# Loads held behind crossbar transposes in a block-sparse attention and MLP-mixer kernel, and two more head pairs turned by the crossbar

## The chip, the cores and the metric

The kernel runs on one core of one Trainium2 chip. The metric is the device time of one execution in microseconds; of several executions the median is taken. TensorE is called PE, VectorE DVE, ScalarE ACT, GpSimd POOL and SyncE SP, as in the profile.

## The reference

The first part is attention over 4 batches of 8 heads, 768 positions and a head size of 64. Positions are grouped in 24 blocks of 32. A query block sees its neighbours, the first and last block, and three sampled blocks; the first and last query block see everything.

```
scores = q @ k.T / 8                      # per batch and head, 768 x 768
scores = where(mask, scores, -1e9)
attn   = softmax(scores)                  # over the keys
x      = concat over heads of attn @ v    # 4 x 768 x 512
```

The second part is a mixer on x: a token step over the 768 positions with 256 hidden units, then a channel step over the 512 channels with 1536 hidden units.

```
u   = x + (relu(x.T @ w_tok1) @ w_tok2).T
out = u + relu(u @ w_ch1) @ w_ch2         # 4 x 768 x 512, float32
```

## The kernel before

The work is cut into 16 **pairs** of heads (pair p has heads 2p and 2p+1; four pairs are a batch). The scores of a pair are made in nine steps: three blocks of 256 queries (t) by three blocks of 256 keys (jj). In a step PE makes the scores of both heads (`ps`, L678), ACT takes their exponential into `et` (L688), and PE multiplies `et` with the values, to which a column of ones is appended (`po`, L772). After the third key block DVE takes the reciprocal of the sum and writes the normalised rows into `x` (L786, L787). In pairs 0 to 3 the mask is added to the scores by 24 additional rows of the operands; from pair 4 on (`NT0`) DVE multiplies `et` by a 0/1 `mask` instead (L696), and the two heads sit in the two halves of the partitions.

There are two score buffers (`ps`), one `po`, seven `et` (`NET`) and three general PSUM buffers (`pm`).

**q and k have to be turned** so that the head dimension lies on the partitions. The rows land in "homes" (`homes`, `load_pair`, L254, DMAs issued by POOL), DVE brings each into the order that the turn wants (`relayout`, L567; v is copied at L564), and then there are two ways. Pairs 1 to `NPE` - 1 are turned by PE against an identity (`transposes`, L620), and DVE or ACT copies the result from PSUM (L634, L649). Later pairs are turned by the DMA crossbar, issued by SP (`crossbar`, L589). With `NPE = 8` pairs 8 to 15 go by crossbar, and their relayouts are planned after `all_loaded`, the landing of the last load. Each turned pair lives in one of four buffers (`NV`) of `ktb` and `qtb`.

**The mixer** runs per batch and half of the channels (g): `tok` (PE L849, L874; DVE L882) and then a turn of u for the channel step, `turn_by_crossbar` (L829, issued by SP). Batch 0 is done pair by pair in `tok_pair` (L909, L932, L940) and turned by PE (L955, evacuated at L966). The channel step is `ch`: its first layer in L989 with the relu on ACT or DVE (L813, L815), its second in L1016, added to u at L1028 and written by SP at L1041.

**The order on each engine** is written by a planner at build time. `Planner` keeps a clock and a list of streams of PE work with priorities (`P.stream`; a lower number goes first) and of single operations (`P.op`) with planned costs. It issues whatever is ready by its own clock. On the chip each engine then runs its instructions in that order, and an instruction waits for its semaphores, with all behind it on that engine. The queue of loads, `pull`, puts POOL's DMAs in order in the same way: pairs 4 to 15 one after the other, `load_ch1` and `load_ch2` after pairs 5 and 7, and the copies that spread the mask (`spread_mask`, L534). From pair 4 on `qk_stream` issues two steps in one visit when it can, which takes two free `ps` buffers and two free `et`.

The head of the program has "filler" matmuls (`idle_mm`, L316), which compute nothing that is used: seven at the start and four of 512 columns just ahead of the first scores.

## Time and profile before

| | us |
|---|---|
| median of 5 executions | 256.38 (255.88 to 257.86) |
| the profiled execution's own time | 257.86 |
| its span, first to last instruction | 255.8 |
| PE busy in it | 247.4 |
| ACT, DVE busy | 176.9, 177.2 |
| POOL busy | 50.1 |

The profile is of one execution, the slowest of the five. Its page gives the busy time of each engine, then the span in 40 slices of 6.4 us, each digit a busy share in tenths. The groups of instructions have the mean duration of one and the idle time ahead of it. [...] what one costs in a row is read from the chain of waits, where a piece "x4" gives the time of four in a row. A timeline line has the start in us, the duration, engine, line, operation, and in brackets the idle time before it and what ended it.

### The profile page before, as it was taken

To read this page: it belongs to the slowest core of one execution; us is meant where nothing else is said; L and a number is where in the kernel's file an instruction comes from. 1 tells how busy PE (TensorE), PEld (TensorE's weight loads), DVE (VectorE), ACT (ScalarE), POOL (GpSimd) and SP (SyncE) were. 2 spreads that over 40 slices of the span, in tenths; PEclk is the share of its full clock that TensorE was granted. 3 is DMA by queue.
4 is the path that set the end of the run, shared out by engine and by line. 5 is a ranking of instruction groups with operands and counts; after the bars stand their busy time and mean duration, and the time that the engine had idled before them with its cause. 6 is when DMAs were issued, how large, how long until landed. Compare 5 with 4: busy or idle time off the path is not lost.

```text
span 255.8 us, 6662 instructions
## 1 busy us (share of the span) xinstructions
PE 247.4 (97%) x2784; PEld 161.2 (63%) x2804; DVE 177.2 (69%) x392; ACT 176.9 (69%) x223; POOL 50.1 (20%) x84
## 2 busy tenths in 40 slices
PE   8899999899999999999999999999999999999995
PEld 2589989656666556656766666557567544556444
DVE  6788968799988988998998998897883113200122
ACT  6699999898989676778978777768775620177100
POOL 8845989477200000000000000000000000000000
PEclk9999999999999999999999999999999999999999
DMA  6999999999947442457050202310410302200123
GB/s 147 196 215 201 213 202 205 203 202 200 201 75 145 79 105 82 61 148 105 3 112 14 62 3 64 82 50 37 103 46 0 64 37 86 109 16 0 41 87 121
DMA packets 43326, 26.36 MB, mean 103 GB/s; under 512 B 23776, under 2 KB 40432, under 8 KB 43296
## 3 DMA queue, kind: packets, MB, share of 16 engines
q0 software_dynamic: 15104, 12.98, 32.0%
q1 hardware_dynamic: 27920, 12.76, 20.2%
q8 instruction: 22, 0.36, 0.6%
q10 hardware_dynamic: 272, 0.20, 0.3%
q14 instruction: 8, 0.07, 0.1%
HBM read 26.74 MB, written 6.29 MB: 129 GB/s over the span
## 4 chain that ended last, share of the span: by engine, by line
PE 89%; DVE 7%; ACT 2%; issue 1%; DVEq 0%; ACTq 0%
PE pm_ch L989 25%; PE pm_ch L1016 24%; PE ps L678 15%; PE po L772 14%; PE pm_tok L874 3%; PE pm_tok L849 3%; PE ps_idle L316 2%; ACT et L688 2%; DVE x L940 1%; DVE et L696 1%; PE pm_tok_p L909 1%; DVE x L787 1%; DVE qlay L567 0%; DVE ktb L634 0%; DVE qtb L419 0%
## 5 line engine op out<-in xcount | busy, mean ns | idle before, releaser
L688 ACT ACTIVATE et<-ps 128x1024 bf16<-128x1024 f32 x144 | 138.9, 1023 | 32.7 <-PE ps L678 30.2
L989 PE MATMUL pm_ch<-uT,w_ch 128*128 128x384 bf16 x384 | 72.1, 326 | 0.0
L696 DVE TENSOR_TENSOR et<-et,mask 128x1024 bf16<-128x1024 bf16 x108 | 69.6, 683 | 0.6 <-ACT et L688 0.6
L1016 PE MATMUL pm_ch<-w_ch,rc 128*128 128x512 bf16 (+2 forms) x292 | 65.9, 362 | 1.1 <-issue 0.5
L772 PEld LDWEIGHTS <-et 128*128 128x128 bf16 x1152 | 49.0, 97 | 17.2 <-issue 2.8
L772 PE MATMUL po<-vaug,et 128*128 128x65 bf16 x1152 | 55.9, 193 | 1.1 <-ACT et L688 0.4
L678 PE MATMUL ps<-qtb,ktb 64*128 64x256 bf16 (+1 forms) x576 | 55.2, 273 | 1.7 <-ACT et L688 1.4
L813 ACT ACTIVATE rc<-pm_ch 128x384 bf16<-128x384 f32 x65 | 32.0, 492 | 25.1 <-PE pm_ch L989 25.0
L989 PEld LDWEIGHTS <-w_ch 128*128 128x128 bf16 x384 | 34.4, 97 | 20.7 <-issue 2.3
L1028 DVE TENSOR_TENSOR o<-pm_ch,x 128x512 f32<-128x512 f32 x23 | 15.9, 690 | 45.1 <-PE pm_ch L1016 45.0
L1016 PEld LDWEIGHTS <-rc 128*128 128x128 bf16 x312 | 27.6, 98 | 25.6 <-issue 1.9
L678 PEld LDWEIGHTS <-ktb 64*128 64x128 bf16 (+1 forms) x576 | 29.5, 95 | 18.8 <-issue 13.7
L787 DVE TENSOR_TENSOR x<-po,recip 128x256 bf16<-128x256 f32 x48 | 20.4, 424 | 1.7
L815 DVE TENSOR_SCALAR rc<-pm_ch 128x384 bf16<-128x384 f32 x31 | 17.1, 553 | 3.0 <-PE pm_ch L989 2.4
L786 DVE RECIPROCAL recip<-po 128x4 f32<-128x4 f32 x48 | 8.6, 180 | 14.4 <-PE po L772 13.7
L882 DVE TENSOR_TENSOR x<-pm_tok,x 128x512 bf16<-128x512 f32 x18 | 11.8, 684 | 3.6 <-PE pm_tok L874 3.4
L874 PE MATMUL pm_tok<-a_t,w_tok 128*128 128x256 bf16 x72 | 10.8, 277 | 0.0
L849 PE MATMUL pm_tok<-x,w_tok 128*128 128x256 bf16 x72 | 9.5, 273 | 0.0
L874 PEld LDWEIGHTS <-w_tok 128*128 128x128 bf16 x72 | 7.5, 128 | 1.7 <-issue 1.1
L534 POOL COPY mask<-maskb 128x240 bf16<-128x240 bf16 (+1 forms) x18 | 8.1, 516 | 0.0
L254 POOL DMA_DIRECT2D vraw<-in_v_dram x10 | 7.5, 750 | 2.9 <-DMA w_ch<-in_moe_w_ch_dram 1.1
L849 PEld LDWEIGHTS <-w_tok 128*128 128x128 bf16 x72 | 6.4, 97 | 1.1 <-issue 0.4
(101 smaller groups left out, 137.2 us busy)
## 6 DMA issues: line engine op xcount, KB each, us to landing
out_dram<-o SPq DMA_DIRECT2D x17, 256.0 KB, 2.0
w_ch<-in_moe_w_ch_dram POOLq DMA_DIRECT2D x8, 384.0 KB, 9.9
vraw<-in_v_dram POOLq DMA_DIRECT2D x10, 192.0 KB, 7.4
kraw<-in_k_dram POOLq DMA_DIRECT2D x9, 192.0 KB, 8.8
qraw<-in_q_dram POOLq DMA_DIRECT2D x9, 192.0 KB, 7.6
out_dram<-o SPq DMA_DIRECT2D x13, 128.0 KB, 2.0
w_tok<-in_moe_w_tok_dram POOLq DMA_DIRECT2D x2, 384.0 KB, 9.7
ktb<-in_v_dram POOLq DMA_DIRECT2D x3, 192.0 KB, 7.3
```

The costliest lines, as they stand in the source:

```text
L678: nc.tensor.matmul(out=ps[:, hd, 256 * i : 256 * i + 256], lhsT=ktb[n][rows, h, 256 * jj + 128 * i : 256 * jj + 128 * i + 128], rhs=qtb[n] ...
L688: nc.scalar.activation(out=et[:, :, :], in_=ps[:, :, :], func=AF.Exp, scale=0.125)
L696: nc.vector.tensor_tensor(out=ets[s][:, :, :].rearrange("k h (i q) -> k h i q", i=2), in0=ets[s][:, :, :].rearrange("k h (i q) -> k h i q" ...
L772: nc.tensor.matmul(out=po[:, hd, c, :], lhsT=et[:, hd, 256 * i + 128 * c : 256 * i + 128 * c + 128], rhs=va[:, hd, 2 * jj + i, 0:65], star ...
L787: nc.vector.tensor_tensor(out=free(xs[b][:, pb // 2, 2 * t, 128 * (pb % 2) : 128 * (pb % 2) + 128], 0, [[64, 2], [256, 2], [1, 64]],), in0 ...
L813: nc.scalar.activation(out=o(), in_=i, func=AF.Relu)
L815: nc.vector.tensor_scalar(out=o(), in0=i, scalar1=0.0, scalar2=None, op0=ALU.max)
L849: nc.tensor.matmul(out=box["pm"][:, t, :], lhsT=w_tok1[:, sc, 128 * t : 128 * t + 128], rhs=xs[b][:, g, sc, :], start=(t == 0 and sc == 0) ...
L874: nc.tensor.matmul(out=ubox["pm"][:, i, :], lhsT=w_tok2[:, t, :, 2 * s2 + i], rhs=a_t[:, t, :], start=(i == 0 and t == 0), stop=(i == 1 an ...
L989: nc.tensor.matmul(out=pbox["pm"][:, 0:384], lhsT=w_ch1[:, dmc, 128 * cc : 128 * cc + 128], rhs=st[b]["uT"][:, dmc // 2, 3 * sh : 3 * sh + ...
L1016: nc.tensor.matmul(out=pbox["pm"][:, 0:n], lhsT=box["rc"][:, cc, 128 * sc : 128 * sc + 128], rhs=w_ch2[:, cc, lo : lo + n], start=(cc == 0 ...
L1028: nc.vector.tensor_tensor(out=o[:, :].rearrange("p (g e) -> p g e", g=2), in0=pbox["pm"][:, :].rearrange("p (g e) -> p g e", g=2), in1=st[ ...
```

## The change

- `NPE` goes from 8 to 6: pairs 6 and 7 are turned by the crossbar too.
- `all_loaded` goes. In its place are `GATES`: behind the loads of pair 7, and again behind those of pair 12, POOL reads one element of each of the two buffers that the crossbar of pair 7 (and 11) writes (`gate`), so that later loads wait for it. The third entry of the table makes no read. Relayouts of a crossbar pair are planned 2 us after the planned end of the loads ahead of the next gate (`quiet`). From pair 9 on a relayout is also planned after the scores of the pair three before.
- SP's planned cost of a crossbar turn goes from 900 to 1300 ns, and what follows it from 5000 to 4600.
- `qk_stream` visits two steps at once only when `mixing()` holds, which is when batch 0 is turned and the channel step can begin.
- The last half of batch 1's u (b = 1, g = 1) is turned by PE and copied from PSUM, not by the crossbar.
- `tok_pair` of pairs 0 to 2 gets a higher priority (stream 2.5 to 1.7, operations 2.2 to 1.5).
- The four fillers of 512 columns ahead of the first scores become eight of 128.

```
--- before.py
+++ after.py
@@ -196,7 +196,8 @@
     NV = 4
     NR = 4
     NET = 7
-    NPE = 8
+    NPE = 6
+    GATES = {7: 7, 11: 12, NP - 1: NP - 1}
     NT0 = 4
 
     sb1 = ctx.enter_context(tc.tile_pool(name="sb1", bufs=1))
@@ -312,10 +313,10 @@
 
     idle_ps = psS.tile([128, 2, 512], FP32, tag="ps", name="ps_idle")
 
-    def idle_mm():
+    def idle_mm(n=512):
         nc.tensor.matmul(
-            out=idle_ps[:, 0, :], lhsT=free(one[:, 0:1], 0, [[0, 128]]),
-            rhs=free(one[:, 0:1], 0, [[0, 512]]), start=True, stop=True,
+            out=idle_ps[:, 0, 0:n], lhsT=free(one[:, 0:1], 0, [[0, 128]]),
+            rhs=free(one[:, 0:1], 0, [[0, n]]), start=True, stop=True,
         )
 
     for i in range(7):
@@ -424,8 +425,8 @@
     first_lay(acopy, "k", 0)
     e2a, e2b = e2_mm(0, psM, "pm"), e2_mm(0, psO, "po")
     kt0 = first_turn("k", 0)
-    for i in range(4):
-        idle_mm()
+    for i in range(8):
+        idle_mm(128)
     first_evac(acopy, "q", 0, 0, qt0)
     first_evac(acopy, "q", 0, 1, qt0)
     e2_copy(acopy, 0, 0, e2a)
@@ -551,7 +552,8 @@
     kT_there, qT_there, va_there, qk_done, pv_done = {}, {}, {}, {}, {}
 
     copied = {}
-    all_loaded = Ev()
+
+    quiet = [Ev() for _ in GATES]
 
     def relayout(p):
         lays = {}
@@ -575,7 +577,9 @@
             if nm != "v" and p >= 3:
                 deps.append(qT_there[p - 2, 1])
             if nm != "v" and p >= NPE:
-                deps.append(all_loaded)
+                deps.append(quiet[sum(p > g for g in GATES)])
+            if nm != "v" and p > NV + 4:
+                deps.append(qk_done[p - NV + 1])
             lays[nm + "ev"] = P.op(("dve",), {"dve": 320.0}, deps, emit, prio=2 if nm != "v" else 3)
             copied[nm, p] = lays[nm + "ev"]
         va_there[p] = lays["vev"]
@@ -591,7 +595,7 @@
                     in_=lays[nm][:, :, :, :].rearrange("p c h d -> p (c h d)"),
                 )
             deps = [lays[nm + "ev"], mask_there, qk_done[p - NV]]
-            ev = P.op(("sp",), {"sp": 900.0}, deps, emit, prio=1, lat=5000.0)
+            ev = P.op(("sp",), {"sp": 1300.0}, deps, emit, prio=1, lat=4600.0)
             there[p, 0], there[p, 1] = ev, ev
 
     def transposes(p):
@@ -733,7 +737,7 @@
 
 
             visit = [s]
-            if todo and (todo[0][1:] != (0, 0) or (todo[0][0], 1) in qT_there):
+            if todo and (todo[0][1:] != (0, 0) or (todo[0][0], 1) in qT_there) and mixing():
                 visit.append(todo.pop(0))
             evs = [(Ev(), Ev()) for _ in visit]
 
@@ -888,13 +892,40 @@
             alias(rel, ev)
             u_evs.append(ev)
         alias(a_rel, last)
-        turn_by_crossbar(b, g, u_evs)
+        if (b, g) != (1, 1):
+            turn_by_crossbar(b, g, u_evs)
+            return
+
+        for dmc in (2 * g, 2 * g + 1):
+            last, rel, tbox = Ev(), Ev(), {}
+            for sc in range(NC):
+                def emit(sc=sc, dmc=dmc, rel=rel, tbox=tbox):
+                    if sc == 0:
+                        P.take("pm", rel)
+                        tbox["pt"] = psM.tile([128, NC, 128], BF16, tag="pm", name=f"pm_ut_{b}_{dmc}")
+                    nc.tensor.matmul(
+                        out=tbox["pt"][:, sc, :],
+                        lhsT=st[b]["u"][:, g, sc, 128 * (dmc % 2) : 128 * (dmc % 2) + 128],
+                        rhs=ident[:, :], start=(sc == 0), stop=(sc == NC - 1), is_transpose=True,
+                    )
+                yield 56.0, [u_evs[sc // 2]], [("pm", 1)] if sc == 0 else [], emit, last if sc == NC - 1 else None
+
+            def evac(eng, dmc=dmc, tbox=tbox):
+                o, i = st[b]["uT"][:, g, :, dmc % 2, :], tbox["pt"][:, :, :]
+                if eng == "act":
+                    nc.scalar.copy(out=o, in_=i)
+                else:
+                    nc.vector.tensor_copy(out=o, in_=i)
+
+            ev = P.op(("dve", "act"), {"dve": 555.0, "act": 740.0}, [last], evac, prio=0.5)
+            alias(rel, ev)
+            alias(st[b]["uT_there"][dmc], ev)
 
     def tok_pair(p):
 
         g, cols = p // 2, slice(128 * (p % 2), 128 * (p % 2) + 128)
 
-        urgent = 0.5 if p == 3 else 2.2
+        urgent = 0.5 if p == 3 else 1.5
         box = {}
         last, rel = Ev(), Ev()
         for sc in range(NC):
@@ -1071,11 +1102,12 @@
     P.stream(0, qk_stream())
     P.stream(1, pv_stream())
     P.stream(2, tr_stream())
-    P.stream(2.5, first_tok_stream((0, 1, 2)))
+    P.stream(1.7, first_tok_stream((0, 1, 2)))
     P.stream(0.5, first_tok_stream((3,)))
     P.stream(3, tok_stream())
     P.stream(4, ch_stream())
     P.stream(1.8, mask_stream())
+
 
 
     loads = deque()
@@ -1087,6 +1119,17 @@
             loads.append(load_ch2)
         if 5 <= p <= 7:
             loads.append(spread_mask(p - 5))
+        for gate, behind in GATES.items():
+            if p == behind:
+                loads.append(("gate", gate))
+    gate_t = {"t": 0.0}
+    gates_seen = []
+    seen = sb1.tile([1, 2], BF16, name="seen")
+
+    def gate(p):
+        for i, buf in enumerate((ktb, qtb)):
+            nc.gpsimd.tensor_copy(out=seen[0:1, i : i + 1], in_=buf[p % NV][0:1, 0, 0:1])
+        gate_t["t"] = qT_there[p, 1].t
 
 
     tenant = {n: n for n in range(NR)}
@@ -1101,7 +1144,17 @@
     def pull():
         while loads:
             x = loads[0]
-            if callable(x):
+            if x == ("gate", NP - 1):
+                quiet[-1].t = dma["free"] + 2.0 * US
+            elif isinstance(x, tuple):
+                still = [e for e in quiet if e.t is None]
+                if still and x not in gates_seen:
+                    still[0].t = dma["free"] + 2.0 * US
+                    gates_seen.append(x)
+                if (x[1], 1) not in qT_there or qT_there[x[1], 1].t is None:
+                    return
+                gate(x[1])
+            elif callable(x):
                 if maskb_there.t is None:
                     return
                 x(max(P.now, maskb_there.t))
@@ -1113,10 +1166,8 @@
                 if not free_from:
                     return
                 t, home = min(free_from)
-                load_pair(x, t, home)
+                load_pair(x, max(t, gate_t["t"]), home)
                 tenant[home] = x
-                if x == NP - 1:
-                    all_loaded.t = arrive["v", x].t
             loads.popleft()
 
     while P.streams or P.ops:
```

## Prediction

> I call step p.k the k-th (0 to 8) of the nine score blocks of pair p; four score matmuls make one step. "V" is the po matmuls, "cut" the multiplication of et with the mask.

> **What bounds the kernel now.** First the page's busy line and its slices of the span.

> ```profile
> PE 247.4 (97%) x2784; PEld 161.2 (63%) x2804; DVE 177.2 (69%) x392; ACT 176.9 (69%) x223; POOL 50.1 (20%) x84
> ...
> PE   8899999899999999999999999999999999999995
> ...
> DVE  6788968799988988998998998897883113200122
> ACT  6699999898989676778978777768775620177100
> ```

> TensorE looks full throughout, but a busy PE isn't PE at its peak, so I cut the span where the mixer's channel matmuls begin (54.4 us) and where the last scores are issued (188.4).

> ```profile
> 0.00:54.40 54.40, 50.50 (x742) 40.63 (x744) 44.01 (x118) 47.41 (x54) 41.13 (x72) 1.00 1.17 198
> 54.40:188.40 134.00, 132.54 (x1645) 84.06 (x1661) 118.30 (x249) 105.50 (x123) 9.01 (x13) 1.00 0.46 90
> 188.40:253.50 65.10, 64.36 (x407) 36.49 (x405) 14.93 (x27) 24.03 (x47) 0.00 (x0) 1.00 0.16 53
> ```

> The columns are length, then PE, PEld, DVE, ACT and POOL busy, clock, DMA share, GB/s. After 54.4 PE is 99% busy and the others are not: there the kernel is worth what PE has to issue. Before that I price PE's work by start-to-start spacing from the chain of waits: a score matmul 0.11 us in pairs 0 to 3 (x4 in 0.44) and 0.068 later (x8 in 0.54), a V matmul 0.031 (x16 in 0.49), a 128-column one 0.055 (x6 in 0.34), a 384-column one 0.1625 (x96 in 15.60). Up to 54.4 this makes about 41 us, so PE has slack, while ACT is busy 94% between 12 and 50. The timeline of ACT:

> ```profile
> 45.89 1.94 ACT L688 ACTIVATE et<-ps 128x1024 bf16<-128x1024 f32 x2 [0.68 <-PE ps L678]
> 47.71 0.39 ACT L813 ACTIVATE a_t_p<-pm_tok_p 128x256 bf16<-128x256 f32 x1
> 48.36 1.94 ACT L688 ACTIVATE et<-ps 128x1024 bf16<-128x1024 f32 x2 [0.26 <-PE ps L678]
> 50.19 0.81 ACT L634 COPY qtb<-tq 128x768 bf16<-128x768 bf16 x1
> 50.87 5.88 ACT L688 ACTIVATE et<-ps 128x1024 bf16<-128x1024 f32 x6
> ```

> Exponentials follow each other at 0.97 us except around pair 4, where ACT waits twice for double score visits (0.68, 0.26) and runs two copies. So **the first 54 us are set by exponentials and what delays them, the rest by PE's remaining work**. What counts is how much PE work is left when the mixing begins. The chain there:

> ```profile
> 54.45 0.67 PE ps L678 x8
> 55.11 0.43 PE pm_ch L989 x2
> 55.55 0.24 PE po L772 x8
> 55.79 1.46 PE pm_ch L989 x9
> 57.25 0.54 PE ps L678 x8
> ```

> By counting score matmuls (176 before 54.3), the first line is steps 4.8 and 5.0, the last 5.1 and 5.2: 57.25 is my reference point. Last, the start:

> ```profile
> 5.61 1.91 PE L316 MATMUL ps_idle<-one 128*128 128x512 bf16 x4
> 7.31 1.06 PE L678 MATMUL ps<-qtb,ktb 88*128 88x256 bf16 x4
> ```
> ```profile
> 6.00 0.74 DVE L405 COPY ktb<-tkfirst 64x384 bf16<-64x384 bf16 x2
> ```

> The scores' last operand is ready at 6.74, and they start at 7.31, behind the fillers.

> [...] the chain has four fillers in 1.71 us (427 ns each), and half-rate matmuls until about 9 us. [...]

> **The change, part by part.**

> Fillers: eight of 128 columns at half rate are 8 x 0.107 = 0.85 us against 1.71. They end near 6.66, the operand is there at 6.74, so scores start near 6.9: **0.4 us earlier**, and the first exponential with them (it waited 1.84 us for PE). [...]

> Pairs 6 and 7 by crossbar: 24 transposes leave PE (24 x 0.055 = 1.32 us) and four copies of 0.55 leave DVE and ACT, one being ACT's 0.81. The four relayouts (0.27 to 0.35) stay, but stand in DVE's order behind cut 4.2. On SP four transposes come (1.25 us to issue each) and one goes (the x of batch 1, second half); SP sits empty from 13 to 74 us, so this costs nothing. Crossbar landing was 2.5 to 3.2 us. First relayout near 52.5, four transposes 1.3 apart: the last lands near 59.5. Step 6.0 came at 68: covered by 8 us; the price if not, 1 for 1.

> Batch 1, second half, by PE: 12 x 0.055 = +0.66 us where PE is the bound, and two copies of 0.55 on DVE, which has 12% free there (0 to 0.3 us).

> Held loads: GpSimd gets four one-element reads (nearest row: an iota of 0.14), nothing on any path, but the loads of pair 8 on queue behind the first two. Before, the first of these was issued at 41.6; now near 59.7. The ch2 weights are ahead of the hold (last issue 38.4, at most 11.3 to land: 49.7), so crossbars find the DMA engines free. The value load of pair 8 is needed first: its copy on DVE moves from ahead of cut 5.1 to ahead of cut 5.7, near 68. An idle queue landed its first load 4.7 us after issue, and the spacing is 0.97: 59.7 + 4.7 + 2 x 0.97 = 66.3. Covered by about 2 us. The second hold (crossbar of pair 11, relayout at cut 8.6) precedes value 13, needed at cut 10.1: 13 cuts, some 17 us for about 10. Nothing.

> Order: tokens of batch 0 ahead of transposes (1.7 for 2.5), single visits until the mixing, later relayouts from pair 9. Between exponential 3.8 and the mixing ACT no longer has its two copies, and single visits need one free score buffer, not two. Before: 45.2 to 54.8 for eight exponentials (50.87 + 4 x 0.97). After: 45.2 - 0.4 + 8 x 0.97 = 52.6; I take 52.8 for new small stalls (0 to 0.8). Steps 4.8 and 5.0 thus go out near 52.9, not 54.45.

> Then DVE decides. In its order cut 4.3 and 4.4 now stand behind uT, two cuts, four relayouts, a normalisation and three relus. Following each by its duration: uT until 51.0, cuts 52.2, relayouts and normalisation 53.9, relu 54.4, 54.9, cut 55.5, relu 56.1, cut 4.4 at 56.7; V 4.4, two 384-column matmuls, then 5.1 at **57.7** (57.2 to 59). Meanwhile PE issues channel matmuls. The order shows that when 5.1 goes out, 20 more of these are done than before and 8 V matmuls fewer: 20 x 0.1625 - 8 x 0.031 = 3.0 us ahead. The 24 dropped transposes lie behind both kernels at that point (before has issued them, the changed kernel never will); the 12 new ones still come: 3.0 - 0.66 = **2.34 us less to do**.

> Sum: -2.34 + (57.7 - 57.25 = 0.45) = -1.9; later DVE copies and other small waits +0.2: **-1.7 us**. The profiled execution is 257.86 with a span of 255.8 and would become 256.2 with 254.1. It was the slowest of five, 1.48 above the median; taken from the median of 256.38: **254.7**.

> **Rivals.** A run of this kernel can tell about 0.5% (1.3 us) from no change: below 255.1 is faster, above 257.7 slower.
> 1. [...] Steps 0.1 to 0.3 and the first V, some 1.9 us of work, then take twice that, less 0.8 us that PE waited anyway: +1.1, so 255.8. For it: [...] the five times lie in two groups (255.9 to 256.4, 257.7 to 257.9). [...]
> 2. DVE's queue at the start of the mixing. Cut 4.3 behind four relayouts and relus that wait for PE: if cut 4.4 ends later, V 4.3 and 4.4 stop PE in order once the three pm buffers are full. It decides from 5.1 at 59.6 (57.25 + 2.34); at 60.9 the kernel is 1.3 us slower; I put it at 258.0. For it: DVE is 95% busy from 50 to 60. Against: 3 us of channel work cover it.
> 3. Held loads late: value 8 landing after 68 stops DVE and, two steps on, PE. If it lands at 71, +3 gives 257.7.
> 4. The change doesn't do what it says: crossbars land before GpSimd reaches its reads, and PE's transposes were in slack. Only +0.66 against the fillers' 0.4: 256.6. Against: GpSimd is at its reads by about 41 us.

> **Numbers.** Forecast 0.56 (own range 253.0 to 255.1); rival 1 0.17, rival 2 0.14, rival 3 0.07, rival 4 0.06. Faster 0.56; same 0.23 (1 and 4); slower 0.21 (2 and 3). Range 253.0 to 258.0.

> **What would show it.** First exponential at 8.0; no ACT copy between 45 and 52; 4.8 near 52.9; the last crossbar of pair 7 at 59.5 with its GpSimd read just after; 5.1 between 57.2 and 59; PE's run after the last scores about 60 us, not 65. Wrong if 5.1 comes after 59.6, if half-rate matmuls go on past 9.5, or if the copy of value 8 waits for a DMA.

## Result: the work saved is there, and TensorE's clock takes it back

The changed kernel takes 257.76 us in the median of 43 executions (254.57 to 260.35). The kernel before, measured beside it in 80 executions, takes 257.25 (255.83 to 261.66). The ratio is 0.9964, with a 95% interval of 0.9943 to 0.9984: under half a per cent, so no change by the bound of the prediction. The forecast was 254.7.

The times of the changed kernel lie in three groups with nothing between them: 254.57 to 255.41 (17 executions), 257.66 to 258.32 (13) and 259.08 to 260.35 (13). With 17 of 43 in the first group, the median falls into the lower part of the second. The ratio leaves out executions more than 1.5% above a kernel's fastest, and so the whole third group. The profiled execution, 259.74 us with a span of 258.0, belongs to that group. It shows what happens there, and an execution of another kernel (e4 below) shows the first group.

The page of the changed kernel: busy time by engine, and the span in 40 slices.

```profile
span 258.0 us, 6661 instructions
...
PE 250.3 (97%) x2777; PEld 163.4 (63%) x2796; DVE 179.7 (70%) x399; ACT 173.3 (67%) x214; POOL 50.8 (20%) x88
...
PE   8998999999999999999999999999999999999995
...
DVE  6746774799889988899889989897998423200222
ACT  6659999987989576877887867667877410177100
```

PE has seven instructions fewer than before and is busy 2.9 us longer. ACT, busy 3.6 us less in all, has 5 in its third slice, where before had 9. The same stretches as before, cut at 54.4 and 188.4 us (length, busy time of PE, PEld, DVE, ACT and POOL, clock, DMA share, GB/s):

```profile
0.00:54.40 54.40, 51.65 (x686) 41.29 (x688) 37.41 (x107) 45.67 (x51) 32.09 (x60) 1.00 1.01 175
54.40:188.40 134.00, 132.59 (x1635) 84.43 (x1651) 119.31 (x250) 103.49 (x122) 18.72 (x28) 1.00 0.59 102
188.40:256.00 67.60, 66.03 (x465) 37.65 (x465) 22.99 (x43) 24.12 (x43) 0.00 (x0) 1.00 0.15 53
```

In the first stretch PE did 686 matmuls where before did 742, and was busy 1.2 us longer with them. The timeline of PE in the first 22 us tells why (start, us, instruction, count; matmuls in a row overlap, and after the four scores of 0.60 us at 19.30 the next matmul starts at 19.73):

```profile
5.61 1.06 PE L317 MATMUL ps_idle<-one 128*128 128x128 bf16 x8
6.46 1.16 PE L682 MATMUL ps<-qtb,ktb 88*128 88x256 bf16 x4
...
8.62 1.89 PE L682 MATMUL ps<-qtb,ktb 88*128 88x256 bf16 x8
...
12.46 1.04 PE L682 MATMUL ps<-qtb,ktb 88*128 88x256 bf16 x4
...
17.70 1.06 PE L682 MATMUL ps<-qtb,ktb 88*128 88x256 bf16 x4
...
19.30 0.60 PE L682 MATMUL ps<-qtb,ktb 88*128 88x256 bf16 x4
```

Four score matmuls take 1.0 to 1.2 us up to 17.7 and 0.60 from 19.3 on: PE runs at half rate until then (in e3 below, where the clock record says half, four take 1.04 to 1.06). The clock record has full rate from 19.27. In the profiled execution of before it has it from 9.46. (The page's clock row shows full rate from the beginning, because it has no record ahead of the first switch: there the durations tell the rate.) The scores of pair 1 start at 21.33 us, against 18.25 before. The short fillers did bring the first scores forward, to 6.46 from 7.31, and the first exponential to 7.66 from 8.41. All of that was gone by pair 1.

What the change was forecast to save is there. From the start of the last scores (195.06, before 188.38) to the end of PE's last matmul (254.82, before 252.99) it takes 59.8 us where before took 64.6; the prediction said 60 and 65. About half of these 4.8 us is work done earlier in the span; the work saved, counted further down, is 2.4 us.

### The profile page after: what moved, and what is told of

The parts are those of the page before. It is cut to its first block, busy times and chain, and to the rows that moved or that the text cites. A ratio compares the mean times of both kernels' runs of the same rounds, so it can differ in the third digit from the quotient of the medians.

```text
span 258.0 us, 6661 instructions
## 1 busy us (share of the span) xinstructions
PE 250.3 (97%) x2777; PEld 163.4 (63%) x2796; DVE 179.7 (70%) x399; ACT 173.3 (67%) x214; POOL 50.8 (20%) x88
## 4 chain that ended last, share of the span: by engine, by line
PE 91%; DVE 4%; ACT 3%; issue 2%; ACTq 0%
PE pm_ch L1020 25%; PE pm_ch L1047 24%; PE ps L682 17%; PE po L776 14%; PE pm_tok L878 3%; PE pm_tok L853 3%; ACT et L692 3%; PE pm_tok_p L940 1%; PE pm_tok_p L963 1%; PE pm_e L413 0%; DVE vaug L566 0%; PE tq L624 0%; DVE ktb L653 0%; PE tk L624 0%; DVE dkf L357 0%
## 5 line engine op out<-in xcount | busy, mean ns | idle before, releaser
L1020 PE MATMUL pm_ch<-uT,w_ch 128*128 128x384 bf16 x384 | 74.1, 326 | 0.0
L776 PEld LDWEIGHTS <-et 128*128 128x128 bf16 x1152 | 52.0, 99 | 17.8 <-issue 2.5
L776 PE MATMUL po<-vaug,et 128*128 128x65 bf16 x1152 | 58.4, 195 | 1.2 <-ACT et L692 0.4
L682 PE MATMUL ps<-qtb,ktb 64*128 64x256 bf16 (+1 forms) x576 | 58.6, 280 | 1.0 <-ACT et L692 0.7
L1020 PEld LDWEIGHTS <-w_ch 128*128 128x128 bf16 x384 | 33.7, 97 | 20.0 <-issue 3.4
L817 ACT ACTIVATE rc<-pm_ch 128x384 bf16<-128x384 f32 x58 | 28.5, 492 | 26.3 <-PE pm_ch L1020 26.0
L819 DVE TENSOR_SCALAR rc<-pm_ch 128x384 bf16<-128x384 f32 x38 | 21.1, 555 | 6.0 <-PE pm_ch L1020 5.5
L878 PEld LDWEIGHTS <-w_tok 128*128 128x128 bf16 x72 | 7.5, 128 | 2.0 <-issue 1.4
L535 POOL COPY mask<-maskb 128x240 bf16<-128x240 bf16 (+1 forms) x18 | 7.2, 482 | 0.0
## 6 DMA issues: line engine op xcount, KB each, us to landing
out_dram<-o SPq DMA_DIRECT2D x17, 256.0 KB, 2.0
w_ch<-in_moe_w_ch_dram POOLq DMA_DIRECT2D x8, 384.0 KB, 10.1
```

The lines of the kernel that those rows point to most:

```text
L682: nc.tensor.matmul(out=ps[:, hd, 256 * i : 256 * i + 256], lhsT=ktb[n][rows, h, 256 * jj + 128 * i : 256 * jj + 128 * i + 128], rhs=qtb[n] ...
L776: nc.tensor.matmul(out=po[:, hd, c, :], lhsT=et[:, hd, 256 * i + 128 * c : 256 * i + 128 * c + 128], rhs=va[:, hd, 2 * jj + i, 0:65], star ...
L817: nc.scalar.activation(out=o(), in_=i, func=AF.Relu)
L819: nc.vector.tensor_scalar(out=o(), in0=i, scalar1=0.0, scalar2=None, op0=ALU.max)
L878: nc.tensor.matmul(out=ubox["pm"][:, i, :], lhsT=w_tok2[:, t, :, 2 * s2 + i], rhs=a_t[:, t, :], start=(i == 0 and t == 0), stop=(i == 1 an ...
L1020: nc.tensor.matmul(out=pbox["pm"][:, 0:384], lhsT=w_ch1[:, dmc, 128 * cc : 128 * cc + 128], rhs=st[b]["uT"][:, dmc // 2, 3 * sh : 3 * sh + ...
```

## Experiments

Of the kernels that start from the changed one, all but e3 and e12 have the four long fillers of before in place of the eight short ones, so that the parts can be compared without that edit; where it is not shown in a diff, the text says so. "Late" below means 3.8 us or more above the kernel's own lowest time. Each was measured in five rounds beside the kernel before, whose medians in these batches were 256.41 (e1 to e4, 11 executions), 257.41 (e5 to e8, 59) and 257.29 (e9 to e12, 66); each batch was on another chip.

### e1 and e2: the fillers alone, in both directions

In e1 the changed kernel has before's four long fillers; e2 is before with the eight short ones.

```
e1, on after:                      e2, on before:
-    for i in range(8):            -    for i in range(4):
-        idle_mm(128)              -        idle_mm()
+    for i in range(4):            +    for i in range(8):
+        idle_mm()                 +        idle_mm(128)
```

> The changed kernel with the four fillers of 512 columns put back; all else as changed. Theory C (clock): [...] full clock comes late (19.3 us in the profile of the changed kernel, 9.5 us in that of before); the rest of the change is worth about -1.3 us. Then this kernel has full clock by about 9.5 us in most executions and a median of 254.8 to 255.8, below both. Theory D (DVE's queue): the loss is at the start of the mixing and the clock is chance: the median stays near the changed kernel's 257.8 and step 5.1 comes 3 us or more after the place that the same start would give.

> The kernel before with only the fillers changed to eight of 128 columns. Theory C: the start is 0.4 to 0.8 us earlier but full clock comes late in a good part of the executions; times in groups 1.5 to 4 us apart, median 0.5 to 2 us above before. Theory D: 0.4 us faster than before in all executions, no new groups.

e1: median 255.60 (254.65 to 260.12, 6 executions), ratio 0.9955 (0.9901 to 1.0008). e2: median 260.04 (256.35 to 261.14, 6), ratio 1.0018 (0.9949 to 1.0087); three of its six were late, and its profile has the clock at full rate from 20.25 us. e1's median lies in the range of Theory C, and e2's lies further above before than the 0.5 to 2 us that the theory gave. That points at the short fillers. But the profiled execution of e1, with the long ones, was late too (20.27 us, span 258.4), so **long fillers do not exclude the late clock**. The two profiles are a pair at the same clock: spans of 258.4 and 259.1, although e1 starts its scores 0.86 us later (7.31 and 6.45).

### e3: twice the fillers

Eight fillers of 512 columns ahead of the first scores, to keep PE busy for longer.

```
     for i in range(8):
-        idle_mm(128)
+        idle_mm()
```

> The changed kernel with eight fillers of 512 columns: twice the filling of before. Theory C: full clock by about 9.5 us in nearly all executions, so the times draw together (spread under 1.5 us); the first scores come 0.85 to 1.7 us later than with four, and the median is that much above the best group of the changed kernel: 255.5 to 256.5. Theory D: 1.7 us above the changed kernel's 257.8.

Median 257.61 (255.10 to 260.63, 6), ratio 0.9997 (0.9940 to 1.0055). The narrow spread did not come. The profile shows full rate from 4.25 us, half rate from 11.08 to 17.91, and full rate after it. Its timeline of PE:

```profile
13.41 1.04 PE L682 MATMUL ps<-qtb,ktb 88*128 88x256 bf16 x4
...
16.93 1.06 PE L682 MATMUL ps<-qtb,ktb 88*128 88x256 bf16 x4
...
18.26 0.60 PE L682 MATMUL ps<-qtb,ktb 88*128 88x256 bf16 x4
```

So there is a second way to lose the clock: it is granted early, and **taken back** for 6.83 us.

### e4: no reads by GpSimd, so that no load is held

```
 def gate(p):
...
-        for i, buf in enumerate((ktb, qtb)):
-            nc.gpsimd.tensor_copy(out=seen[0:1, i : i + 1], in_=buf[p % NV][0:1, 0, 0:1])
```

(with e1's long fillers)

> The first of these four without GpSimd's reads of the turned buffers, so that the loads of pairs 8 on are not held. If the hold costs and gains nothing (C and D alike): within 0.4 us of the first one, the crossbar's landing at most 1 us longer while loads run. If the hold protects the crossbar: landings of 5 us and more, and 1 us or more slower.

Median 254.80 (254.58 to 259.23, 6), ratio 0.9916 (0.9873 to 0.9960). Five of six lie within 0.5 us, and the profiled execution has full clock from 4.27 us with a span of 253.0. Without the hold the crossbar transposes of pairs 6 and 7 are issued while loads run: the page has 168 to 196 GB/s in the three slices from 50.6 to 69.6 us, where the changed kernel has 24 and 101 from 51.6 to 64.5. SP's queue in e4:

```profile
51.00 1.33 SPq L593 DMA_TRANSPOSE ktb<-klay  x1
52.44 2.02 SPq L593 DMA_TRANSPOSE qtb<-qlay  x1
54.64 3.63 SPq L593 DMA_TRANSPOSE ktb<-klay  x1
58.38 5.21 SPq L593 DMA_TRANSPOSE qtb<-qlay  x1
```

The fourth takes 5.21 us to issue. From issue to landing, e4's transposes of q and k need:

```profile
DMA to landing us min/median/max: 2.7/3.6/15.0
```

The same group in the changed kernel, where loads are held:

```profile
DMA to landing us min/median/max: 2.8/3.0/4.8
```

**The hold does what it is made for**, and it buys no time here: e4's lowest time, 254.58, equals the changed kernel's 254.57. In e4 the second transpose, the last of pair 6, lands 12.0 us after its issue, at 64.5, and step 6.0 starts at 67.21; the third lands at 69.7 and pair 7 starts at 78.07 (the trace has no landing for the fourth). The slack covers it. Transposes next to loads have a price in time, with the longest landing going from 4.8 to 15.0 us, and this kernel has the slack to hide it.

### e5, e6, e7: one part of the change undone

e5 gives pairs 6 and 7 back to PE (and holds no load between the crossbars), e6 has double visits back before the mixing, and e7 turns the last half of batch 1's u by crossbar again. All three have e1's long fillers.

```
e5:
-    NPE = 6
-    GATES = {7: 7, 11: 12, NP - 1: NP - 1}
+    NPE = 8
+    GATES = {NP - 1: NP - 1}
e6:
-            if todo and (todo[0][1:] != (0, 0) or (todo[0][0], 1) in qT_there) and mixing():
+            if todo and (todo[0][1:] != (0, 0) or (todo[0][0], 1) in qT_there):
e7:
-        if (b, g) != (1, 1):
-            turn_by_crossbar(b, g, u_evs)
-            return
+        turn_by_crossbar(b, g, u_evs)
+        return
```

> The changed kernel with the four 512-column fillers, and pairs 6 and 7 turned by TensorE again, loads not held (crossbar from pair 8, after all loads, as before). Executions with full clock from about 4.3 us compared (the lowest group of each kernel): with everything changed but the fillers this group is at 254.6 to 255.2, before at 255.9 to 256.5. If the two pairs' crossbar carries the gain of the order: 255.9 to 256.8 (1.32 us of transposes and the 0.66 of the new ones back on TensorE). If the order around them does: 254.6 to 255.4.

> The changed kernel with the four 512-column fillers and double score visits from pair 4 on, as before. If the single visits carry the gain: lowest group 0.5 us or more above 254.6 to 255.2, with ACT waits of 0.5 us and more around pair 4. If they are worth nothing: within 0.3 us.

> The changed kernel with the four 512-column fillers and the second half of batch 1 turned by the crossbar. By the prediction TensorE's turn costs 0.66 us where TensorE is the bound, so this is 0.4 to 0.9 us below 254.6 to 255.2. If the crossbar's place in SP's queue was the limit, it is above.

| | executions | median | lowest | late | ratio |
|---|---|---|---|---|---|
| e5 | 15 | 257.51 | 256.04 | 4 | 0.9980 (0.9945 to 1.0015) |
| e6 | 22 | 256.70 | 255.31 | 4 | 0.9957 (0.9928 to 0.9985) |
| e7 | 22 | 256.65 | 254.31 | 3 | 0.9942 (0.9909 to 0.9976) |

The medians are moved by how many executions lose the clock, so I read the parts from the lowest times, against 254.6 of the whole change (e1, e4 and the changed kernel agree within 0.08). The two pairs by crossbar (with their hold) carry 256.04 - 254.6 = 1.4 us. Two profiles with full rate from the same time, 20.27 us, say nearly the same: a span of 259.6 in e5 and of 258.4 in e1. Single visits carry 0.7, with ACT waits of 0.46 and 0.45 us around pair 4 in e6, and the turn on PE costs 0.3, a little less than the 0.4 to 0.9 expected. These are not terms of one sum, because the planner writes a new order each time. The tokens' priority and the planned waits were not tried alone.

### e8: the fillers put where PE is otherwise empty

Sixteen fillers of 512 columns, not seven, at the very start; the rest as e1.

```
-    for i in range(7):
+    for i in range(16):
         idle_mm()
```

> The changed kernel with the four 512-column fillers, and 16 instead of 7 at the very start, so that TensorE is dense from 1.0 to about 7 us. [...] it comes by 8 us in every execution, none has the first score steps at half rate, and the times lie within 2 us of each other, all later by the 2 to 3 us that the first turn waits: 256.5 to 258. If full clock comes by chance: groups up to 5 us apart as before.

The first of these two forecasts has full clock by 8 us in every execution because PE is dense from the start.

Median 259.87 (256.25 to 261.33, 14), ratio 1.0008 (0.9957 to 1.0059). The profile has full rate from 3.71 us on and a span of 254.6. But nine of the fourteen executions had a mean clock of 0.985 to 0.987 and took 259.69 or more; three of e3's six had such a mean too. With the 0.50 that e3's record shows while the clock was taken back, a mean of 1.4% below full is half rate for 2.8% of the span, 7 us: by this estimate the clock was granted and then taken back for about 7 us in these nine, as in e3 for 6.83. None of the fourteen is late with a mean clock near 1, as the third group of the changed kernel is. So more fillers ahead bring the clock early (3.71 us here, 4.25 in e3) and do not keep it: **they do not help the time**, and the suspicion falls on the gaps that follow them, which e9 to e12 try.

### e9, e10, e11, e12: fillers in the gaps

Ahead of step 0.3 PE waits for an exponential: 0.67 us in e4, whose clock is early, and 0.26 in the changed kernel at half rate. Ahead of step 0.1 I expected a gap of 0.3 us; the changed kernel's profile shows none to speak of there. Here fillers of 256 columns go into these two places: one and two in e9, two and four in e10 (both with e7's edit and e1's long fillers), one and two in the kernel before (e11) and in the changed kernel, short fillers and all (e12).

```
 (ahead of step 0.1)
+            for i in range(1):
+                idle_mm(256)
 ...
+        if s == (0, 1, 0):          # ahead of step 0.3
+            fill = psO.tile([128, 512], FP32, tag="po", name="po_fill")
+            for i in range(2):
+                nc.tensor.matmul(
+                    out=fill[:, 0:256], lhsT=free(one[:, 0:1], 0, [[0, 128]]),
+                    rhs=free(one[:, 0:1], 0, [[0, 256]]), start=True, stop=True,
+                )
```

> The changed kernel with four 512-column fillers and the batch-1 turn by the crossbar (e7), and three more fillers of 256 columns: one ahead of step 0.1 and two ahead of step 0.3, where TensorE waits for DVE and ACT. Theory C: [...] Then the executions that fall back to half rate for 6.8 us (clock 0.986) and those that get full clock only at 20 us become rare, and the median comes to 254.5 to 255.5. If the groups come by chance: a spread as in e7, median 256 to 257.

> As the one before, with twice the filling in both gaps. Theory C: groups as there or fewer, but the filling is now longer than the gaps at half rate: lowest group 0.1 to 0.5 us higher. By chance: as e7.

> The kernel before with only the three gap fillers. Theory C: the groups at 258.8 and 261.5 become rare, median 256.0 to 256.6 against 257.3. By chance: unchanged median.

> The changed kernel as it is, with the eight fillers of 128 columns, and the three gap fillers. Theory C: fewer late grants than the changed kernel's one in three, median below its 257.8; [...] not as good as the first of these four. Theory D: unchanged at 257.8.

| | executions | median | range | late | ratio |
|---|---|---|---|---|---|
| e9 | 22 | 255.45 | 254.14 to 257.88 | 0 | 0.9937 (0.9905 to 0.9969) |
| e10 | 16 | 255.74 | 254.25 to 256.40 | 0 | 0.9935 (0.9908 to 0.9962) |
| e11 | 22 | 257.86 | 256.15 to 261.48 | 1 | 1.0001 (0.9971 to 1.0031) |
| e12 | 18 | 255.11 | 254.62 to 259.17 | 1 | 0.9936 (0.9906 to 0.9967) |

e9, e10 and e12 came out as Theory C expected: e9's median lies in its range, and e10's lowest time is 0.1 us above e9's. e12 is the test of the cause: it is the changed kernel, and three matmuls that compute nothing take its median from 257.76 to 255.11, with one late execution in 18 where there were 13 in 43. Against before, measured beside it, it gains 0.64%; the changed kernel itself was measured in another batch, and before's medians in the two batches are 257.29 and 257.25. e9 is the same comparison with long fillers: it is e7 and the gap fillers, with a median of 255.45 against 256.65. e12's lowest time, 254.62, is that of the changed kernel: the fillers save no work, and what they change is the clock. The profiled execution is one of its middle ones (257.13 us, full rate from 13.49). Its timeline of PE:

```profile
8.62 0.39 PE L317 MATMUL ps_idle<-one 128*128 128x256 bf16 x1
...
10.73 0.63 PE L680 MATMUL po_fill<-one 128*128 128x256 bf16 x2
11.19 1.02 PE L691 MATMUL ps<-qtb,ktb 88*128 88x256 bf16 x4
...
14.25 0.61 PE L691 MATMUL ps<-qtb,ktb 88*128 88x256 bf16 x4
```

The two fillers stand where PE waited for an exponential, and full rate is there by 14.25, five microseconds sooner than in the changed kernel's profile. At half rate the three are not free: steps 0.1 and 0.3 go out at 9.07 and 11.19, against 8.62 and 10.76 in the changed kernel's profile.

e11 missed: in before the same fillers bring no lower median. Late executions did become rare, 1 of 22 against 16 of 66 of before beside it, but eight of the 22 lie at 258.6 to 259.1, which its profile (one of the lowest, full rate from 5.09 us) does not explain. Their mean clock is near 1, so it was not taken back in them; they lie 2.5 to 2.9 us above the lowest, as e12's profile does with a clock from 13.49. That theirs came as late is not shown. So the remedy is shown for the changed kernel's family of orders only.

## Why the prediction was wrong, step by step

**The fillers, "0.4 us earlier", is the step that failed, and rival 1 with it.** The sum had the fillers' gain in full and nothing for the clock. The first scores came even earlier than forecast (6.46, forecast 6.9). In executions with an early clock that gains nothing: the lowest times are 254.57 with short fillers and 254.65 and 254.58 with long ones (e1, e4). The forecast priced both kinds at half rate, and the price held: the eight short ones take 0.85 us in the changed kernel (5.61 to 6.46), the four long ones 1.71 in before's chain of waits. In e4's profile full rate is there ahead of them, and the record of the four long ones is 1.03 us long, that of the eight short ones at half rate 1.06 in the changed kernel:

```profile
5.17 1.03 PE L317 MATMUL ps_idle<-one 128*128 128x512 bf16 x4
6.08 0.89 PE L682 MATMUL ps<-qtb,ktb 88*128 88x256 bf16 x4
```

On the cost side I had rival 1, a clock that comes later and leaves steps 0.1 to 0.3 at half rate for +1.1 us, with a chance of 0.17. That the fillers bear on it was an estimate: before's profile shows one switch to full rate, at 9.46 us, and not what brought it. One of the signs of being wrong that I had named, half-rate matmuls past 9.5 us, is what the profile shows. The measured cost is several times the 1.1. The same order on PE, matmul for matmul but for the fillers, ends at 253.0 with full rate from 4.27 us (e4), at 255.4 from 13.49 (e12) and at 258.0 from 19.27 (the changed kernel): **+2.4 and +5.0 us**. The start of pair 1 carries it: 16.68, 19.08 and 21.33 us, and after it all three run in parallel (steps 1.0 to 15.8 take 173.39, 173.30 and 173.73). The start of pair 1 in e4 and in e12:

```profile
16.68 1.04 PE L682 MATMUL ps<-qtb,ktb 88*128 88x256 bf16 x8
```
```profile
19.08 1.04 PE L691 MATMUL ps<-qtb,ktb 88*128 88x256 bf16 x8
```

I had priced steps 0.1 to 0.3 alone; at half rate the exponentials wait for PE through the whole of pair 0, as ACT's timeline in the changed kernel shows for steps 0.5 and 0.6:

```profile
15.24 1.02 ACT L692 ACTIVATE et<-ps 128x1024 bf16<-128x1024 f32 x1 [0.68 <-PE ps L682]
17.18 1.02 ACT L692 ACTIVATE et<-ps 128x1024 bf16<-128x1024 f32 x1 [0.91 <-PE ps L682]
```

And the chance: 26 of the changed kernel's 43 executions are in the two later groups.

Did the short fillers raise that chance? The mean clock that is on record for each execution tells the two losses apart. It is near 1 where the clock came late, because nothing is recorded ahead of the first switch (the changed kernel's profile has 1.000, with its first record at 19.27), and 0.979 to 0.987 where it was granted and taken back (e3's profile has 0.986).

| | executions | late, mean clock near 1 | mean clock 0.979 to 0.987 |
|---|---|---|---|
| changed kernel (short fillers) | 43 | 13 | 9 |
| long fillers: e1, e4, e5, e6, e7 | 71 | 11 | 6 |
| more fillers ahead: e3, e8 | 20 | 0 | 12 |
| gap fillers: e9, e10, e12 | 56 | 0 | 1 |
| before, beside e1 to e12 | 136 | 29 | 17 |
| before with short fillers: e2 | 6 | 3 | 0 |
| before with gap fillers: e11 | 22 | 1 | 0 |

The step to the gap fillers is plain. It depends a little on where "late" begins: five of e9's 22 lie 3.4 to 3.7 us above its lowest, just under the bound, and its profile, which is one of them, has full rate from 13.26 us. The step from long to short fillers, 17 of 71 to 22 of 43, is indicated rather than settled: the batches were on different chips, before loses the clock in 46 of 136 with its long fillers, and e1 shows that the long fillers can be late too.

The middle group of the changed kernel, 13 of 43, was in no profiled execution. In nine of the 13 the mean clock is 0.987, so there the clock was granted and taken back, as in e3. In the other four it is 0.998, and when it came in them stays open. The changed kernel thus loses time in both ways: by a late grant in its third group, and by one that did not hold in most of its second.

**The starting point was a mixture too.** I subtracted from a profiled execution whose clock came at 9.46 us, and carried the difference to a median of five. Before has groups of its own: 37 of 80 executions within 1.3 us of its lowest, 13 late. A difference of 1.7 us is less than the 2.2 us between the changed kernel's first two groups, and before's own times spread over 5.8 us, so the median could move by where it fell among the groups.

**The order was forecast right in its mechanism, and nearly in size.** To see it, both kernels have to be compared at the same clock. e4 (the whole change but reads and fillers) has full rate from 4.27, e11 (before with gap fillers) from 5.09. The chain of waits of e4, start, length, work:

```profile
51.61 0.54 PE ps L682 x8
52.16 2.54 PE pm_ch L1020 x15
...
54.94 0.97 PE pm_ch L1020 x6
...
56.16 0.32 PE pm_ch L1020 x2
56.48 0.54 PE ps L682 x8
```

And of e11:

```profile
52.94 0.67 PE ps L687 x8
53.60 0.43 PE pm_ch L998 x2
...
54.28 1.46 PE pm_ch L998 x9
55.74 0.54 PE ps L687 x8
```

The first line of each is steps 4.8 and 5.0, the last 5.1. By the matmuls' starts, steps 4.8 and 5.0 go out at 51.55 against 52.87, 1.3 us earlier; the forecast was 1.55 with the fillers' 0.4, 1.15 without. Step 5.1 goes out at 56.42 against 55.67, 0.75 later; forecast 0.45, or 0.85 without the fillers. In between stand 15 + 6 + 2 = 23 channel matmuls, where e11 has 11. With those ahead of step 5.0 it is 31 against 11 when 5.1 goes out, and 328 V matmuls against 336: the 20 more and 8 fewer of the forecast. From 5.1 to PE's last matmul it is 193.4 against 195.8 us, **2.4 less to do; forecast 2.34**. The spans are 253.0 and 254.3: -1.3, and the sum without the fillers was -1.3. Some of this may come from e11's clock, which came 0.8 us later: the lowest spans that were seen are 252.9 and 253.8. At a clock as late in both (e1 and e2, at 20.27 and 20.25) the difference is -0.7, with 0.86 us of longer fillers on e1's side. In time, the lowest of the two kernels are 254.57 and 255.83, -1.3. Of that some 0.3 us lies outside the span (259.74 - 258.0 = 1.7 after, 257.86 - 255.8 = 2.1 before), which I had taken as unchanged; why it changed stays open. So the order is worth 0.7 us of span (with the longer fillers against it) to 1.3 in these pairs, and the forecast of 1.3 is at the upper end.

**ACT without its two copies.** The timeline of ACT after:

```profile
45.17 10.62 ACT L692 ACTIVATE et<-ps 128x1024 bf16<-128x1024 f32 x11
55.75 0.49 ACT L817 ACTIVATE rc<-pm_ch 128x384 bf16<-128x384 f32 x1
56.98 1.94 ACT L692 ACTIVATE et<-ps 128x1024 bf16<-128x1024 f32 x2 [0.73 <-DVE x L791]
```

Eleven exponentials follow each other without a gap at 0.97 us, where before had two waits and two copies. That is the forecast of this stretch, shifted by the late clock.

**Rival 2 (DVE's queue at the start of the mixing) is out.** Step 5.1 comes 61.41 - 46.44 = 14.97 us after step 3.8, and 14.97 in e4 as well; forecast 57.7 - 43.0 = 14.7. In e4 it comes at 56.42, well before the 59.6 from which that rival decided; the 61.41 of the changed kernel's profile is past that sign only because its whole start is late.

**Rival 3 (held loads late) is out.** POOL's timeline after:

```profile
62.18 0.18 POOL L1131 COPY seen<-ktb 1x1 bf16<-1x1 bf16 x1 [20.82 <-DMA ktb<-klay]
63.47 0.68 POOL L1131 COPY seen<-qtb 1x1 bf16<-1x1 bf16 x1 [1.11 <-DMA qtb<-qlay]
...
65.54 0.73 POOL L255 DMA_DIRECT2D vraw<-in_v_dram  x1
```

POOL waits 20.82 us for the crossbar, the loads behind its reads wait with it, and it issues the value load of pair 8 at 65.54; the copy that needs it runs at 73.76 and waited for nothing. The second read was forecast 16.5 us after step 3.8 (59.5 - 43.0, where 43.0 is before's 43.37 less the fillers' 0.4) and came 17.0 after it.

**Rival 4 (the change does not do what it says) is out**, by that wait and by e5. The turn on PE was charged with 0.66 us and cost 0.3 (e7).

## What to carry to other kernels

Before a filler is shortened, or a gap opened, in a kernel's first 20 us, look at the times of many executions and not at one profile: here one order ends at 253.0, 255.4 or 258.0 us by when TensorE's clock comes. Try fillers in the gaps in which TensorE waits anyway, which here did more than fillers ahead of them (medians of 255.11 to 255.74 in e9, e10 and e12, 257.61 and 259.87 in e3 and e8); it held for the changed kernel's order and not for before's. Compare two orders only at the same clock, or by their lowest groups. A saving of 1 us behind such a start is real, and can be invisible in the median until the start is steady.

## What the runs showed of the hardware

```profile
12.44:15.86 3.42, 3.42 (x36) 2.79 (x34) 1.09 (x4) 2.03 (x3) 2.16 (x4) 1.00 1.22 219
15.86:19.27 3.41, 3.41 (x38) 2.91 (x36) 1.68 (x5) 1.85 (x3) 1.41 (x2) 1.00 1.17 213
```

PE was busy for the whole of both, at half rate; the clock came at the end of the second and not of the first. In e8 it came at 3.71 us, when PE had run for 2.71 us, from 1.00 on, and only fillers of 512 columns.

The clock was kept in e4 after this stretch:

```profile
7.68:11.10 3.42, 2.58 (x31) 1.73 (x31) 3.24 (x8) 2.96 (x4) 2.91 (x5) 1.00 1.22 187
```

and taken back in e3 after this one:

```profile
7.67:11.08 3.41, 2.47 (x22) 1.30 (x20) 3.19 (x8) 3.08 (x4) 2.91 (x5) 1.00 1.24 194
```

2.58 us of 3.42 kept it and 2.47 of 3.41 did not, with 31 matmuls against 22. In the fourteen profiles full rate first came between 3.7 and 5.1 us (e3, e4, e8, e11), at 9.5 to 9.8 (before, e6, e7, e10), 13.3 to 13.5 (e9, e12) or 19.3 to 20.3 (the changed kernel, e1, e2, e5), and at no other time. The groups of times fit this. The scores here use 88 of 128 rows and the V matmuls 65 columns; whether that matters was not tried, and what decides stays open.
